# One PSUM tile and one eviction per weight product, and eight layout copies spread over other steps

## Chip, cores, metric

One NeuronCore of one Trainium2 chip. The metric is the device time of one execution in microseconds; the times given are medians of several executions.

TensorE is written PE, VectorE DVE, ScalarE ACT, GpSimd POOL, as in the profile. The names in its lines: tq_ps holds transposes of q, k_ps and v_ps the sorted k and v, s_ps scores, e their exponentials, o_ps attention outputs, x these normalised, h_ps and g the inner layer of the maxout before and after its relu, out_ps the result, wc_ps a piece of the weight product wc below. A name ending in _ps is a PSUM tile. A line of a timeline begins with start and length in us; a line of waits ends with us in total, times, longest.

## What is computed

A block-sorted attention for 4 batches x 8 heads x 768 tokens x 64, followed by a maxout layer (the reference, shortened):

```python
def _attn_ref(q, k, v, sort_net):
    P = sort_net
    for _ in range(5):                      # row and column normalising of exp(P)
        ...
    k_sorted = einsum('bhij,bhjcd->bhicd', P, k_b)
    v_sorted = einsum('bhij,bhjcd->bhicd', P, v_b)
    scores = scale * q_b @ k_sb.T           # block by block, 96 x 96
    attn = softmax(scores)
    return attn @ v_sb

def _moe_ref(x, w1, w2, w_out):             # x: 3072 x 512
    return np.maximum(x @ w1, x @ w2) @ w_out
```

The kernel writes max(x W1, x W2) Wout as relu(x (W1 - W2)) Wout + x (W2 Wout). The product W2 Wout, 512 x 512, is made once; it is called wc, and is made in four pieces of 128 rows (dmt 0 to 3).

## The kernel before

PSUM is one pool of four tiles, each 1024 fp32 columns wide. In the built program whoever needs PSUM nearly always takes the tile whose last reader stands earliest, and waits until that reader is done:

```python
psum = ctx.enter_context(tc.tile_pool(name="psum", bufs=4, space=bass.MemoryType.PSUM))
def ps_f32(name):
    return psum.tile([128, 1024], FP32, tag="ps", name=name)
```

Two pieces of wc share a tile and are evicted together:

```python
def w_product(dmt, eng=None):
    m = dmt % 2
    if m == 0:
        wc_ps[0] = ps_f32("wc_ps")
    for fb in range(NFB):
        nc.tensor.matmul(wc_ps[0][:, m * 512 : (m + 1) * 512], w2T[...], wo_sb[:, fb, :],
                         start=(fb == 0), stop=(fb == NFB - 1))
    if m == 1:
        evac(wc[:, dmt - 1 : dmt + 1, :].rearrange("p t n -> p (t n)"), wc_ps[0], 1024, eng=eng)
```

`evac` copies PSUM to SBUF on ACT or DVE, whichever has the smaller load by the kernel's own account. The second half of v (batches 2 and 3, 128 rows) has to be turned from (c, d) to (d, c) order; DVE does it in eight copies ("turns") while batch 1's attention runs between batch 0's output products. VA is one attention output with its normalising (reciprocal `rs`, product `x` on DVE), SC one score tile, TR one transpose of x by DMA:

```python
tns = [lambda c=c: turn(both, c) for c in range(0, BLK, 12)]
VA[1:6] = [(lambda f=f, g=g: (f(), g())) for f, g in zip(VA[1:6], tns)]
TR[0:2] = [(lambda f=f, g=g: (f(), g())) for f, g in zip(TR[0:2], tns[5:])]
SC[7:] = [lambda f=SC[7], g=tns[7]: (f(), g())]
...
steps[-1:] = group(VA[1], TR[0])
steps += VA[2:3] + group(VA[3], TR[1])
steps += group(*rest[:-1]) + VA[4:5] + rest[-1:] + group(VA[5], TR[2])
steps += VA[6:7] + group(VA[7], TR[3])
```

So two turns stand in a row behind VA1 (its own and TR0's), and two behind VA3.

The softmax here doesn't subtract the row's maximum and nothing guards it: scores larger than these inputs give would overflow.

## Time and profile before

| | before |
|---|---|
| median of the three runs given first | 171.54 us (171.15 to 171.66) |
| span of the profiled run | 169.6 us |
| PE busy | 162.3 us (96%) |
| DVE busy | 91.8 us (54%) |
| ACT busy | 80.4 us (47%) |
| wc evictions | 2 on ACT, 1012 ns each |
| turns of both halves | 8 on DVE, 819 ns each |

### The profile page before, as it was taken

What the parts mean: (1) busy time and instruction counts of PE and PEld (TensorE: products, weight loads), DVE (VectorE), ACT (ScalarE), POOL (GpSimd) and SP (SyncE); (2) the same over time, 40 slices, a digit from 0 to 9 for tenths busy, and PEclk for the clock granted to TensorE, in tenths of its full rate; (3) what the DMA queues carried; (4) which work ended last, traced back from release to release, by engine and by line L of the source; (5) the groups of instructions that cost most, each with busy time, mean ns of one, the idle gap of its engine ahead of it and who ended that gap; (6) DMA issues with size and microseconds to landing.
All of it is one profiled execution on the core that took longest, in us unless ns stands there. A gap on an engine that the chain in (4) does not pass through costs nothing.

```text
span 169.6 us, 4551 instructions
## 1 busy us (share of the span) xinstructions
PE 162.3 (96%) x2015; PEld 97.0 (57%) x2015; DVE 91.8 (54%) x198; ACT 80.4 (47%) x98; POOL 25.3 (15%) x40
## 2 busy tenths in 40 slices
PE   7799999999999999999999999999999999999991
PEld 7638766736666554457665545566554546654461
DVE  4979677689245399847674448074552422330040
ACT  3598975756855554046774350446505404312000
POOL 7944372243300000000510000000000000000000
PEclk9999999999999999999999999999999999999999
DMA  3999999999999652994199349930025173000342
GB/s 47 201 206 207 199 207 206 209 202 206 215 220 198 106 170 52 140 238 151 10 199 169 92 126 215 194 120 6 0 50 150 34 203 128 0 0 0 124 157 94
DMA packets 29811, 23.11 MB, mean 136 GB/s; under 512 B 16672, under 2 KB 24736, under 8 KB 29792
## 3 DMA queue, kind: packets, MB, share of 16 engines
q0 software_dynamic: 10304, 12.58, 43.7%
q1 hardware_dynamic: 19200, 10.04, 23.9%
q8 instruction: 16, 0.26, 0.6%
q10 hardware_dynamic: 288, 0.20, 0.4%
q14 instruction: 3, 0.02, 0.0%
HBM read 25.17 MB, written 6.29 MB: 186 GB/s over the span
## 4 chain that ended last, share of the span: by engine, by line
PE 87%; DVE 6%; ACT 3%; DMA 1%; issue 1%
PE out_ps L608 37%; PE h_ps L581 26%; PE o_ps L471 5%; PE k_ps L377 4%; PE s_ps L444 4%; PE wc_ps L559 3%; PE v_ps L398 2%; PE v_ps L419 1%; PE tw_ps L529 1%; PE tq_ps L347 1%; DMA p_sb<-in_sort_net_dram 1%; PE tq_ps L352 1%; DVE colsum L226 1%; PE o_ps L81 1%; PE tx_ps L509 1%
## 5 line engine op out<-in xcount | busy, mean ns | idle before, releaser
L608 PE MATMUL out_ps<-wo_sb,g 128*128 128x512 bf16 (+2 forms) x208 | 48.3, 363 | 0.0
L581 PE MATMUL h_ps<-xT,w_sb 128*128 128x384 bf16 x256 | 44.8, 326 | 0.2 <-ACT g L595 0.2
L581 PEld LDWEIGHTS <-w_sb 128*128 128x128 bf16 x256 | 24.0, 98 | 15.7 <-issue 0.2
L452 ACT ACTIVATE e<-s_ps 96x768 bf16<-96x768 f32 x32 | 24.2, 804 | 16.1 <-PE s_ps L444 15.9
L608 PEld LDWEIGHTS <-g 128*128 128x128 bf16 x208 | 17.5, 97 | 15.3
L595 ACT ACTIVATE g<-h_ps 128x768 bf16<-128x768 f32 x21 | 16.9, 810 | 18.0 <-PE h_ps L581 18.0
L608 PE MATMUL out_ps<-wc,xT 128*128 128x512 bf16 (+2 forms) x104 | 25.0, 362 | 0.0
L103 ACT COPY o<-out_ps 128x1024 f32<-128x1024 f32 x9 | 9.1, 1012 | 30.0 <-PE out_ps L608 25.7
L597 DVE TENSOR_SCALAR g<-h_ps 128x768 bf16<-128x768 f32 x11 | 10.5, 955 | 22.5 <-PE h_ps L581 22.5
L488 DVE TENSOR_TENSOR x<-o_ps,rs 96x512 bf16<-96x512 f32 x32 | 22.0, 687 | 1.1
L482 DVE RECIPROCAL rs<-o_ps 96x8 f32<-96x8 f32 x32 | 6.4, 199 | 20.5 <-PE o_ps L471 20.4
L608 PEld LDWEIGHTS <-xT 128*128 128x128 bf16 x104 | 9.9, 97 | 11.0
L209 DVE COPY v_dc<-v_raw 64x768 bf16<-64x768 bf16 (+2 forms) x18 | 15.4, 897 | 0.1
L471 PEld LDWEIGHTS <-e 96*128 96x128 bf16 x256 | 11.6, 97 | 6.7 <-DVE x L488 0.5
L471 PE MATMUL o_ps<-v_sb,e 96*128 96x65 bf16 x256 | 12.9, 193 | 0.1
L105 DVE CAST v_sb<-v_ps 96x1024 bf16<-96x1024 f32 x7 | 8.5, 1214 | 5.6 <-PE v_ps L398 5.2
L103 ACT CAST v_sb<-v_ps 96x1024 bf16<-96x1024 f32 x9 | 8.9, 1014 | 1.6 <-PE v_ps L419 1.0
L444 PEld LDWEIGHTS <-kT 64*128 64x128 bf16 x256 | 6.0, 94 | 5.4 <-issue 4.6
L444 PE MATMUL s_ps<-qT,kT 64*128 64x96 bf16 x256 | 8.6, 204 | 0.1
L103 ACT CAST kT<-k_ps 128x1024 bf16<-128x1024 f32 x8 | 7.7, 1021 | 1.1 <-PE k_ps L377 1.1
L105 DVE COPY o<-out_ps 128x1024 f32<-128x1024 f32 x2 | 2.4, 1224 | 10.6 <-PE out_ps L608 9.5
L81 PEld LDWEIGHTS <-fill 128*128 128x128 bf16 x109 | 6.9, 120 | 2.2 <-DVE fill L72 1.2
(76 smaller groups left out, 138.4 us busy)
## 6 DMA issues: line engine op xcount, KB each, us to landing
out_dram<-o SPq DMA_DIRECT2D x11, 512.0 KB, 3.1
k_raw<-in_k_dram POOLq DMA_DIRECT2D x12, 256.0 KB, 10.3
q_raw<-in_q_dram POOLq DMA_DIRECT2D x4, 768.0 KB, 12.6
v_raw<-in_v_dram POOLq DMA_DIRECT2D x6, 384.0 KB, 13.8
w_sb<-in_moe_w_dram POOLq DMA_DIRECT2D x3, 512.0 KB, 15.9
wo_sb<-in_moe_w_out_dram POOLq DMA_DIRECT2D x2, 512.0 KB, 18.8
v_raw<-in_v_dram POOLq DMA_DIRECT2D x3, 256.0 KB, 4.9
w_sb<-in_moe_w_dram POOLq DMA_DIRECT2D x2, 256.0 KB, 14.1
```

The costliest lines, as they stand in the source:

```text
L81: nc.tensor.matmul(ps[:, 0:w], w0, fill[:, 0:w], start=True, stop=True)
L103: nc.scalar.copy(out=out_ap, in_=in_ap)
L105: nc.vector.tensor_copy(out=out_ap, in_=in_ap)
L209: nc.vector.tensor_copy(out=dst, in_=src)
L444: nc.tensor.matmul(ps[:, h2 * 512 + ii * 128 : h2 * 512 + ii * 128 + BLK], kT[b][rows, (hp * 8 + i) * BLK : (hp * 8 + i) * BLK + 128], rhs ...
L452: nc.scalar.activation(out=e[:, 0 : 8 * BLK].rearrange("p (t c r) -> p t c r", t=8, r=R), in_=ps[0:BLK].rearrange("p (t f) -> p t f", t=8) ...
L471: nc.tensor.matmul(ps[:, h2 * 512 + ii * 65 : h2 * 512 + (ii + 1) * 65], e[:, (h2 * 4 + ii) * BLK : (h2 * 4 + ii) * BLK + 128], v_sb[:, m0 ...
L488: nc.vector.tensor_tensor(out=x, in0=ov[:, :, :, 0:D], in1=rs.to_broadcast([BLK, 2, 4, D]), op=ALU.mult,)
L581: nc.tensor.matmul(h_ps[t][:, m * 512 : m * 512 + TCH], w1_sb[:, hp, fb * 128 : (fb + 1) * 128], xT[:, b % 2, ch, hp % 2, hp // 2, :], sta ...
L595: nc.scalar.activation(out=g, in_=src, func=AF.Relu)
L597: nc.vector.tensor_scalar(out=g, in0=src, scalar1=0.0, scalar2=None, op0=ALU.max)
L608: nc.tensor.matmul(dst, g_tiles[b, ch, m // 2][:, m % 2, off : off + 128] if m < NFB else xT[:, b % 2, ch, hp % 2, hp // 2, off : off + 12 ...
```

## The change

Its intent: give each product of wc a tile of its own and evict it at once, so that ACT frees PSUM in smaller pieces and earlier; and never let DVE do two turns in a row, so that the normalising of the attention outputs isn't held up.

```diff
     def w_product(dmt, eng=None):
-        m = dmt % 2
-        if m == 0:
-            wc_ps[0] = ps_f32("wc_ps")
+        ps = ps_f32("wc_ps")
         for fb in range(NFB):
             nc.tensor.matmul(
-                wc_ps[0][:, m * 512 : (m + 1) * 512],
+                ps[:, 0:512],
                 ...
-        if m == 1:
-            evac(wc[:, dmt - 1 : dmt + 1, :].rearrange("p t n -> p (t n)"), wc_ps[0], 1024, eng=eng)
+        evac(wc[:, dmt, :], ps[:, 0:512], 512, eng=eng)
@@
-                VA[1:6] = [(lambda f=f, g=g: (f(), g())) for f, g in zip(VA[1:6], tns)]
-                TR[0:2] = [(lambda f=f, g=g: (f(), g())) for f, g in zip(TR[0:2], tns[5:])]
-                SC[7:] = [lambda f=SC[7], g=tns[7]: (f(), g())]
+                for step, n in [((VA, 0), 0), ((VA, 1), 1), ((VA, 2), 2), ((VA, 4), 3), ((TR, 1), 4), ((VA, 5), 5), ((SC, 7), 6), ((VA, 6), 7)]:
+                    step[0][step[1]] = lambda f=step[0][step[1]], g=tns[n]: (f(), g())
```

More of the change, by code (lines that the diff above doesn't have):

```diff
@@ L12 @@
 BF16 = mybir.dt.bfloat16
+TWICE = 1
 @with_exitstack
@@ L205, in turn_v @@
         src = v_raw[rows].rearrange("p (c d) -> p d c", d=D)[:, d0:d1, c0:c1]
-        if eng == "A":
-            nc.scalar.copy(out=dst, in_=src)
-        else:
-            nc.vector.tensor_copy(out=dst, in_=src)
+        for _ in range(TWICE):
+            if eng == "A":
+                nc.scalar.copy(out=dst, in_=src)
+            else:
+                nc.vector.tensor_copy(out=dst, in_=src)
     rowsum = const.tile([G, NB], FP32, tag="rowsum", name="rowsum")
@@ L550, in w2_transposes @@
         return out
-    wc_ps = {}
     def w_product(dmt, eng=None):
-        m = dmt % 2
-        if m == 0:
-            wc_ps[0] = ps_f32("wc_ps")
+        ps = ps_f32("wc_ps")
         for fb in range(NFB):
             nc.tensor.matmul(
-                wc_ps[0][:, m * 512 : (m + 1) * 512],
+                ps[:, 0:512],
                 w2T[:, fb, dmt * 128 : (dmt + 1) * 128],
```

## The prediction

> **What bounds the kernel now.** I read the page's busy table first, then the chain of work that ended last, then the waits of TensorE (PE), and last the timelines of PE, ScalarE (ACT) and VectorE (DVE) around the lines that the diff touches.
>
> ```profile
> PE 162.3 (96%) x2015; PEld 97.0 (57%) x2015; DVE 91.8 (54%) x198; ACT 80.4 (47%) x98; POOL 25.3 (15%) x40
> PE 87%; DVE 6%; ACT 3%; DMA 1%; issue 1%
> ```
>
> TensorE is busy 96% of the span and carries 87% of the chain; DVE and ACT are about half idle. The 6% of DVE in the chain is the Sinkhorn part at the start, which the change leaves alone. So a change that leaves the matmuls as they are can only win back the holes in PE's stream. Those that hang on a buffer after the start are named in the waits of PE, and they are few:
>
> ```profile
> PE h_ps L581 <- ACT g L595: 0.2, 1, 0.2
> PE tq_ps L347 <- ACT wc L103: 0.2, 1, 0.2
> PE tq_ps L347 <- ACT v_sb L103: 0.2, 1, 0.2
> ```
>
> Two of the three stand exactly where the change works: the second batch's q transposes (tq_ps) wait for a PSUM tile that the eviction of a wc pair, or of a v_ps tile, frees. The timeline of PE between 47 and 54 us shows where:
>
> ```profile
> 46.93 1.57 PE L398 MATMUL v_ps<-bd,v_dc 64*128 64x64 bf16 x48
> 48.66 0.83 PE L347 MATMUL tq_ps<-ident,q_pair 128*128 128x128 bf16 x12 [0.16 <-ACT v_sb L103]
> 49.33 1.89 PE L559 MATMUL wc_ps<-wo_sb,w2T 128*128 128x512 bf16 x8
> 51.15 0.51 PE L444 MATMUL s_ps<-qT,kT 64*128 64x96 bf16 x16
> 51.50 0.63 PE L398 MATMUL v_ps<-bd,v_dc 64*128 64x64 bf16 x16
> 52.32 0.83 PE L347 MATMUL tq_ps<-ident,q_pair 128*128 128x128 bf16 x12 [0.19 <-ACT wc L103]
> 53.02 1.24 PE L608 MATMUL out_ps<-wo_sb,g 128*128 128x512 bf16 x5
> ```
>
> The columns are start, length, engine, line. The v group ends at 46.93 + 1.57 = 48.50, the transposes start at 48.66; the second time 52.13 and 52.32. The timeline of ACT in the same stretch names the instructions that free the tiles:
>
> ```profile
> 47.60 1.92 ACT L103 CAST v_sb<-v_ps 96x1024 bf16<-96x1024 f32 x2 [0.49 <-PE v_ps L398]
> 51.25 1.01 ACT L103 CAST wc<-wc_ps 128x1024 bf16<-128x1024 f32 x1 [1.73 <-PE wc_ps L559]
> 52.16 1.51 ACT L452 ACTIVATE e<-s_ps 96x768 bf16<-96x768 f32 x2
> ```
>
> For the turns, the timelines of DVE and PE from 58 us on:
>
> ```profile
> 58.56 0.69 DVE L488 TENSOR_TENSOR x<-o_ps,rs 96x512 bf16<-96x512 f32 x1
> 59.16 1.56 DVE L209 COPY v_dc<-v_raw 128x768 bf16<-128x768 bf16 x2
> 60.64 0.20 DVE L482 RECIPROCAL rs<-o_ps 96x8 f32<-96x8 f32 x1
> 60.88 0.69 DVE L488 TENSOR_TENSOR x<-o_ps,rs 96x512 bf16<-96x512 f32 x1
> ...
> 61.29 0.67 PE L444 MATMUL s_ps<-qT,kT 64*128 64x96 bf16 x16
> ```
>
> Two turns in a row (59.16, 1.56 us) hold back the normalising pair rs and x, and the 16 score matmuls at 61.29 take 0.67 us where the same 16 take 0.51 us at 51.15: the second score tile takes the buffer that this x, ending at 60.88 + 0.69 = 61.57, sets free.
>
> **What the Trainium skill says.** PSUM — Partial Sum Buffer, "The four PSUM rules": one matmul output fits one bank, 512 fp32 columns. The kernel's pool has four tiles of 1024 fp32 columns, two banks each, so all eight banks. A single W2 Wout product (128x512 in the trace) fills one bank: in its own tile the other bank lies empty, and the four tiles are still four. ScalarE: Activation LUTs, "What ACT_TABLE_LOAD costs": an ACTIVATE takes 186 ns plus 0.833 ns per column, and back-to-back ones overlap by some 93 ns. The trace agrees on the slope: ACT copies from PSUM of 256 and 1024 columns take 372 and 1012 ns, (1012 - 372) / 768 = 0.833; and on the overlap, since e starts at 52.16 while the wc eviction ends at 52.26. Perfetto Trace Analysis, "Per-engine timelines": a matmul's end is estimated, a DVE or ACT end is the acknowledged write. So I take PE gaps from starts, and read 52.26 to 52.32 as the time from an eviction's end to the matmul that it frees.
>
> **The change, part by part.** In the built programs PE's instructions stand in the same order in both; so do those of the DMA queues. ACT has four 512-column evictions in place of two of 1024. DVE has the same eight turns at other places. One pair of v_sb evictions swaps its engines (the second of batch 1 goes to DVE, the third to ACT).
>
> *Work on ACT.* A 512-column eviction comes to 372 + 256 x 0.833 = 585 ns (an estimate from the two copies above). Four are 2.34 us against 2 x 1.012 = 2.02: ACT works 0.32 us more. It has 16 us idle before e alone, and none of the 0.32 lies on the path if the queue order holds.
>
> *First wait, 48.66.* Now tq_ps takes the buffer of the first v_ps, which ACT evicts at 47.60 to 48.61. In the changed program tq_ps takes the tile of the third product (dmt 2) instead. That product's matmuls end at about 46.98, ACT is through with the kT evictions at 46.06 + 1.05 = 47.11, so the eviction runs to about 47.65, long before PE needs the tile at 48.4. It ends just as the first v_ps is ready for ACT (47.60), so the v evictions are not held up. What PE gains: without a wait the same passage from v to transposes exists at 16.05 and 17.43 us, where the transposes start 0.05 and 0.07 us before the modelled end of v. Here they start 0.16 us after it. 0.16 + 0.06 = **0.22 us**.
>
> *Second wait, 52.32.* tq_ps takes the buffer of the last wc eviction. At 585 instead of 1012 ns it ends 0.43 us earlier, 51.83 on the old clock. PE could start at 52.13 - 0.06 = 52.07. The wait goes: 52.32 - 52.07 = **0.25 us**. The first out_ps then has its buffer from the first e, which also starts 0.43 us earlier. It now starts 0.13 us before the modelled end of the transposes, the product at 49.33 0.16 us before: **0.03 us** more.
>
> *The turns.* One turn of 128x768 takes 0.82 us. Now there is one between VA1 and VA2, so VA2's x ends some 0.75 us earlier, and the score matmuls lose their wait: 0.67 - 0.51 = **0.16 us**. The first turn moves up behind VA0's x, at 55.7, where DVE sits idle for 2.63 us until 58.32. The last turn moves between VA6 and VA7; VA7's x then ends 0.8 us later, about 71.95 on the old clock. Its tile is next needed by the first h_ps at 72.83, so there is 0.9 us of room.
>
> Elsewhere in 54 to 73 us PE is busy in every part of the stretch, so nothing more is to be won by easing DVE there. After 73 us both programs are the same, and the gain is carried through to the end, since PE sets the end.
>
> Sum: 0.22 + 0.25 + 0.03 + 0.16 = 0.66 us. 171.54 - 0.66 = 170.88, so **170.9 us**, 0.4% less.
>
> **The rivals.**
>
> (a) *The new evictions cost a wait.* On ACT the eviction of dmt 2 stands before the v_sb evictions, and that of dmt 0 before the fourth xT eviction, which ends 0.3 us later (about 37.5). For: 0.32 us more work in a first-in first-out queue. Against: the h products that read this xT start at 38.22, and ACT is idle at 47.1 to 47.6. If wrong, PE waits some 0.3 us at 38 or 48 us: 171.2.
>
> (b) *The first turn waits for its data.* It reads v_raw of batches 2 and 3, and stands on DVE before VA1's normalising. The four loads are issued by POOL at 37.27 to 42.56 and take 12.3 to 14.0 us, so the first halves are there by about 39.24 + 14.0 = 53.2, the last load at 42.56 + 12.5 = 55.1. Turn one starts at about 55.2 and needs first halves only: 2 us of room, and DVE's idle 2.6 us would take another 2. If wrong by much, VA1 and VA2 slip and 0.5 to 1 us is lost: 171.5 or a little more.
>
> (c) *Only holes are filled that a later wait gives back.* PE waits for ACT once more at 118 us (0.2 us), and batch 3's loads are released by an ACT result. All of that hangs on work that moves with PE, so I expect nothing to be given back; if it were, the time stays 171.5.
>
> (d) *More is won than the sum*: DVE's double turn at 63.05 also delays VA4 by about 0.9 us, but the o_ps matmuls at 63.20 and the out_ps ones follow with no hole. Nothing in the trace speaks for more than 0.1 us.
>
> **Range and chances.** The sum has four small terms, three read from a start against an undisturbed start; each may be off by a third. The three runs of before lie 0.5 us apart (171.15 to 171.66), as much as the gain. So 170.3 to 171.5. A gain of 2% would be 3.4 us, while all holes in PE's stream at which the change works come to 0.7; a loss of 2% would need DVE to stall for over 3 us. Faster 0.01, same 0.98, slower 0.01.
>
> **What would show it right or wrong.** In the changed profile: both tq_ps rows gone from the waits of PE; tq_ps starting before the modelled end of v in both places; wc evictions of 128x512 near 585 ns, four of them; the 16 score matmuls after VA3 at 0.51 us; the first turn within 0.2 us after VA0's x; the last product of out_ps earlier by 0.6 to 0.7 us. Wrong would be: a new PE row that waits for ACT or DVE between 36 and 73 us, an event wait on DVE for a DMA before the first turn, or a span that is shorter by 0.66 us at 73 us and not at the end.

## The result

The changed kernel took 170.85 us (median of 6 runs, 170.41 to 171.02), the kernel before 171.41 us (6 runs, 171.05 to 171.66). The ratio is 0.9968, with a 95% interval of 0.9951 to 0.9986. Ratios are the mean time of one kernel's fast runs over that of the other's in the same rounds, so not quite the ratio of the medians. Run again later with five rounds, it gave 170.81 against 171.46 us, ratio 0.9967 (0.9954 to 0.9980). By the rule used here (a difference under 2% counts as none) that is "the same"; by its interval it is faster by about 0.3%. The prediction said 170.9.

The busy times on the page of the changed kernel are nearly those of before:

```profile
PE 161.7 (96%) x2015; PEld 96.7 (57%) x2015; DVE 91.9 (54%) x198; ACT 80.6 (48%) x100; POOL 25.6 (15%) x40
```

Its waits of PE, all that are listed, no longer have a tq_ps row; what is left are waits of the first 22 us and one h_ps:

```profile
PE fill_ps L82 <- DVE late L87: 1.4, 1, 1.4
PE fill_ps L82 <- DVE fill L73: 1.2, 1, 1.2
PE o_ps L82 <- DVE x L490: 0.2, 1, 0.2
PE h_ps L578 <- ACT g L592: 0.2, 1, 0.2
PE pe L288 <- DVE p_bf L230: 0.2, 1, 0.2
```

The timeline of PE in the stretch where the two waits were (line numbers have shifted by two or three):

```profile
46.95 1.57 PE L400 MATMUL v_ps<-bd,v_dc 64*128 64x64 bf16 x48
48.46 0.84 PE L349 MATMUL tq_ps<-ident,q_pair 128*128 128x128 bf16 x12
...
51.31 0.63 PE L400 MATMUL v_ps<-bd,v_dc 64*128 64x64 bf16 x16
51.87 0.84 PE L349 MATMUL tq_ps<-ident,q_pair 128*128 128x128 bf16 x12
52.55 1.46 PE L605 MATMUL out_ps<-wo_sb,g 128*128 128x512 bf16 x6
```

The v group ends at 46.95 + 1.57 = 48.52 and the transposes start at 48.46, before that modelled end; the second time 51.94 and 51.87. The same in the timeline of ACT:

```profile
47.06 0.59 ACT L104 CAST wc<-wc_ps 128x512 bf16<-128x512 f32 x1
47.63 1.94 ACT L104 CAST v_sb<-v_ps 96x1024 bf16<-96x1024 f32 x2
51.06 0.58 ACT L104 CAST wc<-wc_ps 128x512 bf16<-128x512 f32 x1 [1.50 <-PE wc_ps L557]
51.55 1.51 ACT L454 ACTIVATE e<-s_ps 96x768 bf16<-96x768 f32 x2
```

The third product is evicted at 47.06 to 47.65, in the gap that ACT had before the v evictions, and these begin at 47.63 against 47.60 before. And the timelines of DVE and of PE where the turns are:

```profile
54.53 0.69 DVE L490 TENSOR_TENSOR x<-o_ps,rs 96x512 bf16<-96x512 f32 x1
55.14 0.81 DVE L211 COPY v_dc<-v_raw 128x768 bf16<-128x768 bf16 x1
...
58.70 0.82 DVE L211 COPY v_dc<-v_raw 128x768 bf16<-128x768 bf16 x1
59.44 0.19 DVE L484 RECIPROCAL rs<-o_ps 96x8 f32<-96x8 f32 x1
59.67 0.69 DVE L490 TENSOR_TENSOR x<-o_ps,rs 96x512 bf16<-96x512 f32 x1
```

```profile
60.83 0.51 PE L446 MATMUL s_ps<-qT,kT 64*128 64x96 bf16 x16
```

The first turn follows VA0's x at once, one turn stands ahead of VA2's rs, and the 16 score matmuls take 0.51 us.

**A finer measure than the time.** Two executions of one kernel differ by up to about 1 us (1.6 in e6, see there), and the traces show from where: PE's first score matmul starts between 18.58 and 18.88 us, depending on the start-up, and from the start of the last output matmul to the end of the span (the last output DMAs) it is 3.3 to 4.1 us. The two profiles of the changed kernel have 4.00 and 3.76 us there. So I also give the *PE stretch*: from the start of the first score matmul (s_ps) to the start of the last output matmul (out_ps), read from the single instructions of each trace. The two profiles of the changed kernel agree in it to 0.006 us. All the waits in question lie within it. The last column compares with runs of before of the same rounds, whose medians lie between 171.38 and 171.46 us; the row of before has its first six runs.

| run | PE stretch, us | against before | median time, us | ratio to before (95%) |
|---|---|---|---|---|
| before | 147.018 | | 171.41 | |
| changed | 146.369 | -0.649 | 170.85 | 0.9968 (0.9951 to 0.9986) |
| changed, again | 146.363 | -0.655 | 170.81 | 0.9967 (0.9954 to 0.9980) |
| e1 wc part only | 146.532 | -0.486 | 171.14 | 0.9984 (0.9967 to 1.0000) |
| e2 turns only | 146.866 | -0.152 | 171.32 | 1.0002 (0.9985 to 1.0019) |
| e3 shared tile, halves evicted | 147.232 | +0.214 | 171.78 | 1.0026 (1.0011 to 1.0041) |
| e4 one turn moved | 146.864 | -0.154 | 171.19 | 0.9989 (0.9970 to 1.0008) |
| e5 evictions done twice | 146.916 | -0.102 | 171.49 | 1.0008 (0.9988 to 1.0028) |
| e6 turns twice, spread | 150.102 | +3.084 | 175.17 | 1.0225 (1.0191 to 1.0259) |
| e7 turns twice, old places | 151.696 | +4.678 | 176.45 | 1.0295 (1.0276 to 1.0314) |
| e8 changed, two scores in a group | 146.025 | -0.993 | 170.32 | 0.9939 (0.9925 to 0.9954) |
| e9 third and fourth product only | 146.530 | -0.488 | 171.25 | 0.9991 (0.9975 to 1.0007) |
| e10 e8 and k evictions swapped | 145.875 | -1.143 | 170.02 | 0.9920 (0.9907 to 0.9933) |

The times alone don't tell e2, e4, e5 and e9 from before (their intervals hold 1); for these the stretch speaks, from one trace each.

Matching each matmul of the changed kernel with the same one of before shows where the 0.649 us come from. The distance between the two changes by 0.02 us or more at four places only: at the first tq_ps (0.232 us), the second tq_ps (0.242), the first out_ps (0.025) and the second score tile at 61 us (0.143). These are net from place to place, small drifts between them included, and sum to 0.642.

### The profile page after: what moved, and what is told of

The parts are those of the page before. It is cut to its first block, busy times and chain, and to the rows that moved or that the text cites. A ratio compares the mean times of both kernels' runs of the same rounds, so it can differ in the third digit from the quotient of the medians.

```text
span 169.2 us, 4552 instructions
## 1 busy us (share of the span) xinstructions
PE 161.7 (96%) x2015; PEld 96.7 (57%) x2015; DVE 91.9 (54%) x198; ACT 80.6 (48%) x100; POOL 25.6 (15%) x40
## 4 chain that ended last, share of the span: by engine, by line
PE 88%; DVE 6%; ACT 2%; DMA 1%; issue 1%
PE out_ps L605 37%; PE h_ps L578 26%; PE o_ps L473 5%; PE k_ps L379 4%; PE s_ps L446 4%; PE wc_ps L557 3%; PE v_ps L400 2%; PE v_ps L421 1%; PE tw_ps L531 1%; DMA p_sb<-in_sort_net_dram 1%; PE tq_ps L354 1%; PE tq_ps L349 1%; DVE colsum L228 1%; PE o_ps L82 1%; PE tx_ps L511 1%
## 5 line engine op out<-in xcount | busy, mean ns | idle before, releaser
L104 ACT COPY o<-out_ps 128x1024 f32<-128x1024 f32 x9 | 9.1, 1012 | 30.0 <-PE out_ps L605 25.7
L557 PE MATMUL wc_ps<-wo_sb,w2T 128*128 128x512 bf16 x32 | 7.8, 380 | 0.1
```

The source lines that it names most:

```text
L104: nc.scalar.copy(out=out_ap, in_=in_ap)
L557: nc.tensor.matmul(ps[:, 0:512], w2T[:, fb, dmt * 128 : (dmt + 1) * 128], wo_sb[:, fb, :], start=(fb == 0), stop=(fb == NFB - 1),)
```

## The experiments

My theory was the one predicted: three buffer waits, of which two go because a wc tile comes free earlier and one because DVE does one turn instead of two. Rivals: that only one part matters; that the smaller eviction alone would do it; that ACT's or DVE's work as such is the point. All runs gave a correct result.

### e1 and e2: each part alone

e1 is the changed kernel with the turns of before, e2 the changed kernel with the `w_product` of before. The edits are the two hunks of the diff above, one each taken back.

> Only the wc part: own PSUM tile and own eviction for each product, turns as before. Theory (two buffer waits of tq_ps plus a later first e): PE is ahead of the kernel before by 0.23 us at the first tq_ps, 0.47 at the second, 0.50 at the first out_ps, and stays there; the 16 score matmuls near 61 us keep their 0.67 us. Time 0.50 us under before (about 0.3%). Rival (the turns bring most of it, the wc waits are given back later): PE is ahead by less than 0.2 us at the end.

> Only the turns part: turns as in the changed kernel, wc pairs as before. Theory: both tq_ps rows stay in PE's waits, PE is level with before until 61 us, then ahead by 0.14 to 0.16 us, because the 16 score matmuls take 0.51 in place of 0.67 us. The time itself is too close to before to tell by the runs (0.1%). Rival (easing DVE helps in other places of 54 to 73 us too, or the early first turn waits for v_raw): ahead by 0.3 us or more at 73 us, or an idle DVE for a DMA at the first turn.

e1's PE stretch is shorter by 0.486 us, e2's by 0.152. The sum, 0.638, is that of the whole change within 0.011. In e1 the tq_ps rows are gone from the waits and the 16 score matmuls take 0.68 us; in e2 both rows are there and the scores take 0.52. The times agree with e1 (ratio 0.9984); e2's 0.1% is too small for them (1.0002, interval 0.34% wide), so for e2 only the trace speaks.

### e9: the second pair alone

```diff
-        m = dmt % 2
+        m = dmt % 2 if dmt < 2 else 0
...
-        if m == 1:
-            evac(wc[:, dmt - 1 : dmt + 1, :]..., wc_ps[0], 1024, eng=eng)
+        if dmt == 1:
+            evac(wc[:, 0:2, :]..., wc_ps[0], 1024, eng=eng)
+        if dmt > 1:
+            evac(wc[:, dmt, :], wc_ps[0][:, 0:512], 512, eng=eng)
```

> Own tiles and evictions for the third and fourth product alone; the first two stay a pair, turns as before. Theory: the first pair's split wins nothing, since no PE start between 36 and 46 us waits for ACT in either trace; so this run gives the whole of the wc part, 0.50 us at the first out_ps and at the end, like the run with all four split. Rival: the split of the first pair has a share (buffers go round in another order afterwards): less than 0.4 us here.

-0.488 us, against -0.486 with all four split. The first pair's split wins nothing.

### e3: two evictions, but a shared tile

```diff
-        if m == 1:
-            evac(wc[:, dmt - 1 : dmt + 1, :]..., wc_ps[0], 1024, eng=eng)
+        evac(wc[:, dmt, :], wc_ps[0][:, m * 512 : (m + 1) * 512], 512, eng=eng)
```

> Tiles shared by two products as before, but each half evicted by itself; turns as before. It separates the shorter last eviction from the own tile. Theory: the first tq_ps still takes the buffer of the first v_ps and waits for ACT until 48.66 us or 0.03 later; the second tq_ps finds its tile free, since the last half takes 0.585 us, not 1.01. PE ahead by 0.24 at the second tq_ps, 0.27 at the first out_ps and at the end. Rival (what counts is that ACT does the third product's eviction early, not the tile): PE ahead by 0.5 us, as with own tiles.

This one missed. The second pair did as expected: PE gained 0.255 us at the second tq_ps and 0.02 at out_ps, and waited as before at the first. But the kernel as a whole is slower than before (+0.214 us in the stretch, ratio 1.0026). PE lost 0.494 us at the second product, a place that I had not looked at. A row of PE's waits, a line of PE's timeline and one of ACT's, of e3:

```profile
PE wc_ps L559 <- ACT wc L103: 0.3, 1, 0.3
```

```profile
36.72 1.89 PE L559 MATMUL wc_ps<-wo_sb,w2T 128*128 128x512 bf16 x8 [0.33 <-ACT wc L103]
```

```profile
36.08 0.58 ACT L103 CAST wc<-wc_ps 128x512 bf16<-128x512 f32 x1 [0.72 <-PE wc_ps L559]
```

In the timeline of before the same eight matmuls start at 36.20:

```profile
36.20 1.89 PE L559 MATMUL wc_ps<-wo_sb,w2T 128*128 128x512 bf16 x8
```

The first half's eviction runs from 36.08 to 36.66, and only then does PE begin the second half of the same tile. The built program says why: in e3 the second product's first matmul has a semaphore wait for ACT, which the program of before doesn't have. The dependency is kept for the whole tile, although the two halves are 512 fp32 columns each. The Trainium skill, PSUM — Partial Sum Buffer, "PSUM bank collisions raise a hardware error", has the rule to guard PSUM by bank and quadrant; by that page a bank holds 512 fp32 values, so the two halves are two banks, and the wait comes from the program and not from the bank rule. (No run here has PE write one bank of a tile while ACT reads the other.) In the second pair the dependency costs nothing: the first half is evicted from 47.55 to 48.13 us in e3, and PE turns to the second product only after its first tq_ps, which starts at 49.18. In the built program that product has no wait of its own; PE has by then waited for a v_sb eviction that ACT does later. e3 also settles a side effect: splitting the evictions changes the kernel's load account, and two v_sb evictions swap engines (ACT, ACT, DVE becomes ACT, DVE, ACT) in e3 as in the changed kernel. The first tq_ps waits all the same in e3, so the swap is not what removed that wait. So an own tile for each product is not only a way to free a buffer sooner: it is what makes early eviction harmless where the next product follows at once.

### e5: own tiles, each evicted twice

```diff
         evac(wc[:, dmt, :], ps[:, 0:512], 512, eng=eng)
+        nc.scalar.copy(out=wc[:, dmt, :], in_=ps[:, 0:512])
```

> Changed kernel with every product evicted twice from its own tile by ACT (the same values written again; result right). Theory: the first tq_ps is still free of a wait, because the third product's tile is free by about 48.15 us; the second tq_ps waits again, for an eviction that ends at about 52.13 in place of 51.64, so it starts 0.3 us later than in the changed kernel; from there on PE is 0.3 to 0.4 us behind the changed kernel, and ahead of before by about 0.25. Rival (ACT work as such sets the time): 2.3 us more ACT work costs far more than 0.4 us, or also moves the first tq_ps.

The first tq_ps stayed free of a wait (PE's distance to the changed kernel moves by less than 0.02 us there), although ACT had 0.6 us more to do ahead of it. The second one waits again. Lines of PE's and ACT's timelines of e5:

```profile
52.34 0.83 PE L349 MATMUL tq_ps<-ident,q_pair 128*128 128x128 bf16 x12 [0.38 <-ACT wc L565]
```

```profile
51.70 0.58 ACT L565 CAST wc<-wc_ps 128x512 bf16<-128x512 f32 x1
```

The second eviction ends at 52.28 and the transposes start at 52.34, 0.06 us later, as at this place in the kernel before. PE falls 0.547 us behind the changed kernel (146.916 - 146.369), more than the 0.3 to 0.4 that I expected: the wc matmuls themselves start 0.08 us later, because the second eviction also pushes the v_sb eviction that frees their tile, and two evictions in a row take 1.19 us (51.09 to 52.28), not the 1.07 that I had counted. The direction and the place are as the theory has them, the size was off by half. ACT's work as such is not the point: 2.3 us more of it cost 0.55.

### e4: one turn moved

```diff
-TR[0:2] = [(lambda f=f, g=g: (f(), g())) for f, g in zip(TR[0:2], tns[5:])]
+TR[1:2] = [lambda f=TR[1], g=tns[6]: (f(), g())]
+VA[6:7] = [lambda f=VA[6], g=tns[5]: (f(), g())]
```

> Kernel before with one turn moved: the one that stood with the first output transpose goes behind the seventh attention output; wc pairs as before. Theory: only the double turn between the second and the third attention output cost PE anything, so this one move brings the whole of the turn part: the 16 score matmuls after the fourth output take 0.51 us, PE ahead by 0.14 to 0.16 us from there on, level before it. Rival (spreading all of them, or the early first turn, matters): less than 0.1 us.

-0.154 us, the same as all of the turn part in e2 (-0.152), and 0.51 us for the score matmuls. Only the double turn behind VA1 cost PE anything; the double turn behind VA3, which "one to a step" also removes, cost nothing, although it held up VA4's normalising.

### e6 and e7: the turns done twice

```diff
-tns = [lambda c=c: turn(both, c) for c in range(0, BLK, 12)]
+tns = [lambda c=c: (turn(both, c), turn_v(both, "D", c, c + 12)) for c in range(0, BLK, 12)]
```

e6 has this in the changed kernel, e7 in e1 (turns at the places of before).

> Changed kernel with each of the eight turns done twice (same values), 8 x 0.75 = 6 us more on DVE. Theory: DVE has 54 to 73 us of 19 us with 15 busy, and each turn that stands between two attention outputs is in DVE's queue: from VA1 on 7 outputs at 0.83, 7 double turns at 1.48 and the q_pair copies at 0.94 are 17.1 us, so the last x ends at about 75 in place of 70.3 and PE, which needs its tile at 72.2, stands some 2.7 us: time about 173.5. Rival (DVE has slack enough in its queue): under 1 us lost.

> As the run with doubled turns, but with the turns at their places of before (wc as in the changed kernel). No turn lies in DVE's idle stretch before VA1, so the eight double turns come after it: 18.6 us from 57.9 us, the last x ends at about 76.5, PE stands some 4 us: time about 175, 1 to 1.5 us more than with spread turns. If the places don't matter once DVE is the limit, both are alike.

DVE becomes the limit, as expected, and more than expected: e6's stretch is 3.73 us longer than the changed kernel's (I had said 2.7), e7's 5.33 (I had said 4). The largest wait of PE in e6 and two lines of its DVE timeline:

```profile
PE h_ps L578 <- DVE x L490: 2.2, 1, 2.2
```

```profile
58.65 1.70 DVE L211 COPY v_dc<-v_raw 128x768 bf16<-128x768 bf16 x2
60.26 0.20 DVE L484 RECIPROCAL rs<-o_ps 96x8 f32<-96x8 f32 x1
```

A double turn holds DVE's queue for 60.26 - 58.65 = 1.61 us, where I had taken 1.48; seven of them make 0.9 of the 1.0 us that I was short. The difference between the two orders, 151.696 - 150.102 = 1.594 us, is one double turn: the one that e6 does in DVE's idle time before VA1. In both, the h_ps matmuls that PE waits for start about 0.05 us after DVE's last x (75.89 after 75.83 in e6, 77.55 after 77.50 in e7). And in e7 the wait that the turn part removes grows from 0.15 to 1.67 us:

```profile
62.86 0.34 PE L446 MATMUL s_ps<-qT,kT 64*128 64x96 bf16 x8 [1.67 <-DVE x L490]
```

So where DVE is loaded, the new places are worth ten times what they are worth here (1.594 against 0.152 us), and at the end it is the turn in idle time that counts, not the splitting of the pairs.

Something else shows in e7's trace: from 63.26 us on, just after that wait, the granted clock is 0.5 for 3.41 us, and 128x512 matmuls start 0.427 us apart in place of 0.215. It costs nothing at the end, since DVE's queue sets when h_ps may start. In e6 the profile shows no such drop before the last matmul, even after a wait of 2.21 us; but e6's two longer runs (175.74 and 175.99 us, the others 174.41 and 174.60) are those with a mean clock of 0.99 in place of 1.00. What sets it off is not shown. e6's median is therefore less sure than its stretch.

### e8 and e10: the same kind of wait elsewhere

PE's waits of the changed kernel still have an h_ps that waits for ACT's g. Three score tiles in one group hold three of the four PSUM tiles, so the next h_ps must take the fourth, which ACT is emptying. e8 puts two in that group and three in the later one; e10 also fixes the engines of batch 3's k evictions.

```diff
-steps += VA[:1] + group(*SC[2:5]) + VA[1:2]
-rest = SC[4:] if b == 1 else SC[5:]
+steps += VA[:1] + group(*SC[2:4]) + VA[1:2]
+rest = SC[5:] if b == 0 else SC[4:]
```

```diff
-ks = [lambda t=t, b=b: sort_k(b + 1, t) for t in range(3)]
+ks = [lambda t=t, b=b: sort_k(b + 1, t, eng="ADA"[t] if b == 2 else None) for t in range(3)]
```

> The changed kernel once more, unaltered, so that its time stands beside the next two in the same rounds and its size is known better. Theory: PE ahead of before by 0.65 us at the last out_ps counted from the score stage at 20 us; time 0.3 to 0.4% under before, median near 170.8. A rival that the gain is given back at the end (the last output DMA takes longer when it is issued sooner) would show as 0.2% or less.

> Changed kernel plus one more move, to see whether the same kind of hole can be closed elsewhere: in batch 2's part two score tiles stand in the group where three did, the third goes to the next group. In the changed kernel the h_ps at 118.5 us waits for ACT's g (PE waits: 0.2), since all other tiles are held by scores. Expected: that wait goes, PE ahead of the changed kernel by 0.25 to 0.3 us at the end, time about 170.55. Rival: three scores in the later group hold the tiles there and an equal wait comes up near 126 us; time as the changed kernel.

> As the run before, and batch 3's three k evictions go to ACT, DVE, ACT in place of DVE, ACT, DVE. In the changed kernel the scores at 114.1 us start 0.15 us late (0.24 us after the h matmuls where 0.10 is usual), since DVE's second k eviction ends at 113.98. Expected: PE ahead of the changed kernel by 0.35 to 0.45 us at the end, time about 170.4. Rival: the choice of engines for later evictions follows the loads that the scheduler has added up, so g and o evictions move to DVE and a new wait for DVE comes up; time as the changed kernel or worse.

PE's timeline of the changed kernel, then that of e8:

```profile
117.49 0.75 PE L446 MATMUL s_ps<-qT,kT 64*128 64x96 bf16 x24
118.46 1.46 PE L578 MATMUL h_ps<-xT,w_sb 128*128 128x384 bf16 x8 [0.22 <-ACT g L592]
```

```profile
117.46 0.51 PE L446 MATMUL s_ps<-qT,kT 64*128 64x96 bf16 x16
117.91 1.47 PE L578 MATMUL h_ps<-xT,w_sb 128*128 128x384 bf16 x8
```

The wait is gone. PE is 0.513 us ahead from the next matmuls on; 0.17 of it goes back at 126 us, where the third score tile now stands; 0.344 stay (146.369 - 146.025). e10 brings 0.15 us more, at the scores of 114 us, where its change is aimed. Both won a little more than I expected (0.34 and 0.49 us under the changed kernel, against 0.25 to 0.30 and 0.35 to 0.45). The times follow: 170.32 and 170.02 us, against 170.81 for the changed kernel in the same rounds. e10 beats both kernels (ratio to before 0.9920).

## Why the prediction was right

The time (170.9 against 170.85 and 170.81), the range and "same" were right, and so was the sum by its terms. That the time itself agrees to 0.05 us is in part luck: it starts from 171.54, the median of three runs, where six runs gave 171.41, and single runs of before lie 0.6 us apart. The terms don't hang on that:

| step of the prediction | said, us | measured, us |
|---|---|---|
| first tq_ps wait goes | 0.22 | 0.232 |
| second tq_ps wait goes | 0.25 | 0.242 |
| first out_ps earlier | 0.03 | 0.025 |
| score tile's wait goes | 0.16 | 0.143 |
| sum | 0.66 | 0.642 by places, 0.649 by stretch |

- **What bounds it.** PE stayed 96% busy, and its stretch shortened by the sum of the removed waits and nothing else. e5 and e6 show the other side: four more evictions on ACT (4 x 0.58 = 2.3 us) cost 0.55 us, and eight more turns on DVE (8 x 0.82 = 6.6 us) cost 3.7, each only from where its queue reached a matmul's buffer.
- **The wc part.** Both waits went as argued; e9 shows that the third and fourth product do it all. The estimate of 585 ns for the eviction was met (585 ns, mean of the four in the groups by form):

```profile
L104 ACT CAST wc<-wc_ps 128x512 bf16<-128x512 f32 x4 | 2.3, 585 | 3.0 <-PE wc_ps L557 3.0
```

- **The turns.** The place and size of the one wait were right, and e4 shows that one move of the eight suffices. One side step was wrong, without effect: I said that VA7's x would end 0.8 us later because a turn now stands before it. It ends at 69.65 + 0.69 = 70.34 us in the changed kernel, that is 70.34 + 0.65 = 70.99 on the old clock, against 70.44 + 0.69 = 71.13 before, so a little earlier. In both kernels all turns but those done before VA1 stand ahead of VA7 in a queue that is nearly full; moving one of them into the idle time before VA1 takes it out of that queue, which I had not counted.
- **Rival (a), a new wait from the additional evictions**: not in the changed kernel. It is real, though: e3 has it, at the first pair, with 0.49 us, because there the tile is shared.
- **Rival (b), the first turn waiting for v_raw**: the turn starts at 55.14, while x runs to 55.22; no wait.
- **Rival (c), given back later**: not within the stretch. The time from the start of the last output matmul varies by 0.8 us between the traces, which is why single times can't show the 0.65 us; over 6 and 5 runs the medians differ by 0.56 and 0.65.
- **Rival (d), more than the sum**: no. The stretch shortened by 0.649, the places give 0.642, and by e4 the double turn behind VA3 cost PE nothing.

What stays open: why the end, from the start of the last output matmul, takes 3.3 to 4.1 us. It differs between two profiles of the same kernel, so no part of the change is needed to explain it.

## What to carry to other kernels

Where one engine is busy 96% of the time, read the holes in its stream from starts against an undisturbed start of the same pair of instructions; their sum is what a reordering can win, and here it was right to 0.02 us. When pieces of work share a PSUM tile, evict them together or give each its own tile: evicting one half early from a shared tile made the next half wait for the eviction where it followed at once. Extra work for a half-idle engine is free only up to the point in its queue from which a buffer is awaited, so first find the idle gap in that queue (here ACT's 0.5 us at 47 us and DVE's 2.6 us at 55 us) and put the work there.

## What the Trainium skill lacked or had wrong

- ScalarE: Activation LUTs, "What ACT_TABLE_LOAD costs", gives 186 ns plus 0.833 ns per column for an ACTIVATE with immediate scale and bias, and that passage doesn't say which memory it reads. The slope held; the fixed part of the ACT copies and casts from PSUM here is smaller: 585 - 512 x 0.833 = 158 ns at 512 columns, 1012 - 1024 x 0.833 = 159 ns at 1024. Since the skill tells PSUM from SBUF elsewhere, this is a gap of that passage and not shown to be an error.
- TensorEngine Tiling (Array Packing), "Key Properties", says that a change of tiling mode drains TensorE, and gives no time. Going from 128-row products to the 64-row scores cost about 0.10 us in these traces (0.311 us from the last wc matmul to the first score matmul at 51.15, where the wc matmuls stand 0.216 apart; in the trace of before all six passages from an output product to a score matmul take 0.311 or 0.312 as well, and those to the 96-row o_ps products 0.215 or 0.216). That it is the drain is not shown.
- PSUM — Partial Sum Buffer has the guard by bank and quadrant, but not that a program which keeps dependencies by tile, with tiles of two banks, makes PE wait at the other bank too: 0.49 us in e3.
